# Seven visits one product later in their group, and the last head group's first output piece one period later

## The chip, the cores and the metric

The kernel runs on one core of a Trainium2 chip. The metric is the device time of one execution in microseconds (us); smaller is better. Before the change it was 687.55 us, the median of three runs.

## The reference

The program is one transformer block in bf16: sliding-window attention on a normalised input, a residual, and a dense layer with silu on the normalised result, again with a residual.

```python
qkv = x_ln @ wqkv                       # x_ln = layernorm(A_x), (2048, 1024)
q, k, v = 32 heads of 32 columns each
scores = (q @ k.T) * 32 ** -0.5
mask = (idx[:, None] - idx[None, :] >= 0) & (idx[:, None] - idx[None, :] < 256)
o = softmax(where(mask, scores, -1e9)) @ v
h = x + o @ wo
out = h + silu(layernorm(h) @ w1) @ w2  # w1 (1024, 3584), w2 (3584, 1024)
```

## The kernel before

The 2048 rows are four blocks of 512. The 32 heads are eight head groups of four heads; one unit of attention work is a head group `i = 8 * block + group` of one block. TensorE (PE in the profile) is kept busy with the dense products: first q, k and v of the four blocks (`qk_group`, L275, and `v_group`, L265), then the product with `wo` (`wo_group`, L296), then the dense layer (L801 and L829). Each such **group** is eight products of 128x512 into one PSUM bank, which VectorE (DVE) then copies out with a CAST (L277, L267) or an addition (L299).

The attention is threaded through the dense products by hand. The class `Attention` holds two tables, and `between` is called ahead of every dense product with a running count, `seen`: what a table holds for that count is issued first, in PE's own order. A PE instruction that has to wait therefore holds every product behind it.

- A **visit** (`visit`, L404 for its matmuls) computes scores with small matmuls of 32 rows by 64 columns, eight of them side by side, and then has ScalarE (ACT) take the exponential of each bank (L333 `exp_c`, L339 and L340 `exp_xy`, L442 `exp_0`) and GpSimd (POOL) apply the mask (L475). Blocks 1 to 3 are done in pairs of head groups, numbered `p` from 0 to 11. A **period** of 48 products belongs to each pair, from `t = 256 + 48 * p`, and holds three visits, `n` = 0, 1, 2, ahead of products `t+4`, `t+20` and `t+36`.
- A **piece** (`attn_piece`, L485) multiplies the exponentials of half a head group by v. VectorE follows with a reciprocal and a multiplication (L496, L497) that write the normalised output, and after the second half of a head group a transposing DMA is queued for the start of the next dense group (`late`).

Four PSUM banks serve all of that beside the four of `sc`. Three rotate among the dense groups; seen from a visit, `now` holds the group that is half done, `idle` is the bank that the next group will take, `behind` is the bank of the group just finished. The fourth, `out`, takes the results of the pieces and, at a visit, one unit of scores. A visit fills `sc`, `idle` and `out`, and where there is work for it `behind`:

```python
now = acc_n[0] % 3
idle, behind, out = (now + 1) % 3, (now + 2) % 3, 3
```

A first visit (`n` = 0) has a unit for `behind` only while `p < 8`: one head of the last two units of block 0 (`rest`, numbers 14 and 15), which belong to head group `G - 1` = 7. These are the visits with a **seventh bank** (four of `sc`, three more). Within the list of a visit with a seventh bank, the part for `behind` comes in the second half. Each of `rest`'s four heads is ready after two periods, so the two pieces of head group 7 of block 0 stand late: one in period 3 and one in period 7, ahead of product 32 of the period. Where they do, the piece that otherwise stands ahead of product 28 of the period (`t + 76` of the pair before) stands ahead of 27 (`t + 75`).

VectorE also does the layer norms of the next block between the groups: `ln1_steps` gives statistics, a reciprocal root by Newton steps, and four normalisations (`ln_norm`, L234), and the loop over `dense` appends one or two steps after every second group. For block 2 the four normalisations fall after groups 13 and 15, which end at `seen` = 432 and 448; period 3 begins at 400, period 4 at 448. An engine works its instructions in the order in which they were issued.

Of the kernel before, what the change touches and what calls it, by code (L numbers as in the profile page):

```python
# [54 lines left out]
def kernel(  # L55
# [22 lines left out]
    G = H // 4  # L78
# [56 lines left out]
    def xbuf(i):  # L135
        return r_e[:, 3072 + 5120 * (i % 2):5632 + 5120 * (i % 2)]

    def ybuf(i):
        return r_e[:, 5632 + 5120 * (i % 2):8192 + 5120 * (i % 2)]
# [165 lines left out]
    def mid_at(i, bank, h):  # L305
        return (h + 2) % 4 if bank == "X" and i % 2 else h
# [11 lines left out]
    def unit_xy(i, odd):  # L318
        q0 = odd * P
        mid, first, last = odd, odd - 2, odd + 2  # L320
        return [
            [(i, mid, q0, q0 + 320, 64), (i, last, q0 + 256, q0 + 384, 384), (i, first, q0, q0 + 64, 0)],
            [(i, mid, q0 + 64, q0 + 384, 128), (i, first, q0, q0 + 128, 0), (i, last, q0 + 320, q0 + 384, 448)],
        ]

    def unit_c(i):
        pair = (i, i + 1) if (i + 1) % 3 < (i + 2) % 3 else (i + 1, i)
        return [[(ii, kt, q * P, q * P + P, (n * 2 + m) * P)
                 for n, ii in enumerate(pair) for m, (kt, q) in enumerate(((-1, 0), (2, 3)))]] * 2

    def exp_c(i, h, bank):
        lo, hi = sorted(((i + 1) % 3, (i + 2) % 3))
        nc.scalar.activation(out=c_ring[:, lo:hi + 1:hi - lo, h, :], in_=four[bank].rearrange("p (n q) -> p n q", q=256),  # L333
                             func=ACT.Exp, scale=scale)

    def exp_xy(e, banks, h0, h1, m0=0):
        tri, mid = banks[:, :, 0:192], banks[:, :, 192:320]
        tri = bass.AP(tensor=tri.tensor, offset=tri.offset, ap=[*tri.ap[:2], [320, 2], tri.ap[2]])
        nc.scalar.activation(out=tri_of(e)[:, h0:h1, :, 64:256], in_=tri, func=ACT.Exp, scale=scale)  # L339
        nc.scalar.activation(out=full_of(e)[:, m0:m0 + h1 - h0, :], in_=mid, func=ACT.Exp, scale=scale)  # L340

    def select_xy(e, pair):
        four_q = e[:, 1024 * pair:1024 * (pair + 1)].rearrange("p (c q) -> p c q", q=256)
        select(four_q[:, :, 0:P], four_q[:, :, 64:64 + P], False)
        select(four_q[:, :, P:2 * P], four_q[:, :, P:2 * P], True)

    def visit(i, n):


        now = acc_n[0] % 3  # L350
        idle, behind, out = (now + 1) % 3, (now + 2) % 3, 3
        p = (i - G) // 2
        rest = (14 + p % 2, p // 2) if n == 0 and p < 8 else None
        c0, c1 = {1: (0, 2), 2: (1, 3)}.get(p // 2, (1, 2))
        if n == 0:
            own, e_own = unit_xy(i, 0), xbuf(i)
            more = [(c0, idle, unit_c(i)), (c1, out, unit_c(i))]
            if rest:
                more.append((rest[1], behind, unit_0(rest[0])))
        elif n == 1:  # L360
            own, e_own = unit_xy(i, 1), ybuf(i)
            more = [(5 - c1, idle, unit_c(i)), (0, out, unit_xy(i + 1, 0)), (1, behind, unit_xy(i + 1, 0))]
        else:
            own, e_own = unit_xy(i + 1, 1), ybuf(i + 1)
            more = [(1 - c0, idle, unit_c(i)), (2, out, unit_xy(i + 1, 0)), (3, behind, unit_xy(i + 1, 0))]
        scores(own, more, (idle, out)[:2 if n == 0 else 1], bool(rest))
        side = [h for h, _, unit in more if n and len(unit[0]) == 3]
        for h, bank, unit in more:
            if h in side:
                exp_xy(xbuf(i + 1), four[bank].rearrange("p (h q) -> p h q", h=1), h, h + 1, mid_at(i + 1, "X", h))  # L370
            elif len(unit[0]) == 4:
                exp_c(i, h, bank)
            else:
                exp_0(rest[0], h, bank)
        if side:
            select_xy(xbuf(i + 1), side[0] // 2)
        exp_xy(e_own, sc[:], 0, 4)
        for pair in range(2):
            select_xy(e_own, pair)
        if rest:  # L380
            m, h = rest
            select_0(m, h, h + 1)
            if m % 2:
                join_0(m, h, h + 1)

    def scores(own, more, ahead, longest=False):
        todo = []
        for h in range(4):
            for half in range(2):
                runs = [(sc[:, h, :], own[half])]  # L390
                for hh, bank, unit in more:
                    if hh == h:
                        runs.insert(0 if bank in ahead else 1, (four[bank], unit[half]))
                at = -sum(p[3] - p[2] for _, parts in runs for p in parts) if longest else 0
                for bank, parts in runs:
                    for p in parts:
                        todo.append((at, h, half, bank, p))
                        at += p[3] - p[2]
        todo.sort(key=lambda m: (m[0], m[4][2] - m[4][3] if longest else 0))
        for _, h, half, bank, (ii, kt, qa, qb, col) in todo:  # L400
            b, g = divmod(ii, G)
            t = b * 4 + kt
            r0, k0 = h * DH, (t % 4) * P + half * 64
            nc.tensor.matmul(  # L404
                bank[half * 64:half * 64 + 64, col:col + qb - qa],
                lhsT=kT[t // 4][r0:r0 + DH, g, k0:k0 + 64], rhs=qT[b][r0:r0 + DH, g, qa:qb],
                start=True, stop=True, tile_position=(r0, half * 64),
            )

    def unit_0(m):  # L410
        i, odd = divmod(m, 2)
        if odd:
            return [
                [(i, 1, 128, 448, 0), (i, 3, 384, 512, 320), (i, 2, 448, 512, 448)],
                [(i, 1, 128, 512, 0), (i, 3, 448, 512, 384), (i, 2, 448, 512, 448)],
            ]
        return [[(i, 0, 0, 320, 0), (i, 2, 256, 448, 320)], [(i, 0, 0, 384, 0), (i, 2, 320, 448, 384)]]
# [8 lines left out]
    def select_0(m, h0, h1):  # L426
        e = heads_0(m, h0, h1)

        if m % 2:
            select(e[:, :, 0:P], e[:, :, 0:P], True)  # L430
            select(e[:, :, 512:640], e[:, :, 320:448], True)
            select(e[:, :, 256:384], e[:, :, 256:384], False)
        else:
            select(e[:, :, 512:640], e[:, :, 256:384], False)
            select(e[:, :, 0:P], e[:, :, 0:P], True)
            select(e[:, :, 320:448], e[:, :, 320:448], True)

    def join_0(m, h0, h1):
        nc.gpsimd.tensor_copy(out=heads_0(m, h0, h1)[:, :, 384:448], in_=heads_0(m - 1, h0, h1)[:, :, 448:512])

    def exp_0(m, h, bank):
        nc.scalar.activation(out=heads_0(m, h, h + 1)[:, 0, 0:512], in_=four[bank], func=ACT.Exp, scale=scale)  # L442
# [71 lines left out]
    class Attention:  # L514


        def __init__(self):
            self.seen = 0
            self.visits, self.pieces = {}, {}
            at = [108, *range(132, 260, 16)]  # L520
            for k in range(8):
                self.visits[at[k]] = lambda k=k: visit_0(k)
            gaps = (1, 4), (1, 10), (2, 4), (3, 4), (4, 4), (4, 10), (5, 4), (5, 10), (6, 4), (6, 10), (7, 4), (7, 10), (8, 4), (8, 10)
            for d, (k, late) in enumerate(gaps):
                self.pieces[at[k] + late] = (d // 2, d % 2)
            for p in range((NB - 1) * G // 2):
                i, t = G + 2 * p, 256 + 48 * p
                for n in range(3):
                    self.visits[t + 4 + 16 * n] = lambda i=i, n=n: visit(i, n)
                for n in range(4):  # L530
                    self.pieces[t + (42, 47, 59, 75 if p in (2, 6) else 76)[n]] = (i + n // 2, n % 2)
            for k in range(2):
                self.pieces[256 + 48 * (4 * k + 3) + 32] = (G - 1, k)

        def between(self, kt):
            if self.seen in self.pieces:
# [169 lines left out]
    for g0 in range(0, G, 4):  # L706
        for w in range(2):
            for g in range(g0, g0 + 4):
                run_late()
                n = g0 * 2 + w * 4 + g % 4  # L710
# [171 lines left out]
```

## Time and profile before

| | before |
|---|---|
| median of 3 runs | 687.55 us (687.27 to 687.96) |
| the profiled execution's own time | 687.86 us |
| its span, first to last instruction | 686.1 us |
| PE busy | 672.4 us, 98% of the span |
| DVE, ACT, POOL busy | 291.7, 237.2, 163.0 us |
| granted TensorE clock | 1.000 |

A row of the timeline gives the start and the length in us, then engine, line, operation, what is written from what, and how many instructions are merged into the row; in brackets stands idle time of the engine ahead of the row and what ended it. Starts of matmuls are recorded; ends are modelled, and since matmuls are pipelined a row's end can lie after the start of the next. Some matmul records are missing from a trace. In this one a product of 128x512 starts 0.216 us after the one before it wherever nothing intervenes, and a gap of about 0.16 us called "issue" stands where such a record is missing.

### The profile page before, as it was taken

The page shows a single profiled execution, that of the slowest core. Times are in us where ns is not written, and L with a number is a line of the kernel's source. Part 1 is how long each engine was busy: PE and PEld are TensorE (multiplying, and loading weights), DVE is VectorE, ACT ScalarE, POOL GpSimd, SP SyncE. Part 2 cuts the span into 40 slices and gives each one's busy share as a digit, 9 for nine tenths or more (in the row PEclk, how much of TensorE's full clock was granted, in tenths as well). Part 3 has the DMA queues.
Part 4 walks back from the last instruction along what each step waited for, and adds up shares of the span by engine and source line. Part 5 has one row for each costly group of instructions (what it writes and reads, how often), then busy time and mean ns, then how long its engine had stood idle before and what let it go on. Part 6 is the DMA issues. An engine that isn't in the chain of part 4 may idle for free.

```text
span 686.1 us, 14503 instructions
## 1 busy us (share of the span) xinstructions
PE 672.4 (98%) x6097; PEld 338.1 (49%) x6200; DVE 291.7 (43%) x615; ACT 237.2 (35%) x405; POOL 163.0 (24%) x304
## 2 busy tenths in 40 slices
PE   9999999999999999999999999999999999999998
PEld 4445555555555555444444444444444444444445
DVE  5277745764444446634416133342244251344111
ACT  7337567667667674023300033200133100233000
POOL 1027966767776665000000000000000000000000
PEclk9999999999999999999999999999999999999999
DMA  8823124025633589865033310033200123100010
GB/s 275 261 53 89 33 55 102 19 41 90 190 88 70 166 250 266 194 237 189 1 104 113 67 39 1 0 93 78 76 1 0 40 83 86 39 1 0 32 38 24
DMA packets 77617, 61.50 MB, mean 90 GB/s; under 512 B 52464, under 2 KB 60656, under 8 KB 77552
## 3 DMA queue, kind: packets, MB, share of 16 engines
q1 hardware_dynamic: 77408, 60.31, 31.9%
q8 instruction: 48, 0.79, 0.5%
q10 hardware_dynamic: 144, 0.26, 0.1%
q14 instruction: 17, 0.14, 0.1%
HBM read 39.85 MB, written 8.39 MB: 70 GB/s over the span
## 4 chain that ended last, share of the span: by engine, by line
PE 97%; issue 1%; DMA 1%; DVE 0%; SPq 0%
PE hacc L801 16%; PE bank L275 16%; PE hacc L829 15%; PE bank L829 13%; PE bank L801 12%; PE bank L296 8%; PE bank L265 6%; PE bank L485 5%; PE sc L404 2%; PE bank L404 2%; PE bank L618 1%; DMA r_w<-in_A_wqkv_dram 1%; PE tp L265 1%; DVE r_o L234 0%; DVE r_a L277 0%
## 5 line engine op out<-in xcount | busy, mean ns | idle before, releaser
L475 POOL TENSOR_SCALAR_AFFINE_SELECT r_e<-r_e 128x512 bf16<-128x512 bf16 (+3 forms) x255 | 150.5, 604 | 105.6 <-ACT r_e L339 48.6
L829 PEld LDWEIGHTS <-r_a 128*128 128x128 bf16 x952 | 90.9, 98 | 103.0
L801 PEld LDWEIGHTS <-r_w 128*128 128x128 bf16 x896 | 87.7, 98 | 105.7
L829 PE MATMUL hacc<-r_a 128*128 128x512 bf16 (+2 forms) x523 | 103.2, 356 | 0.5
L829 PE MATMUL bank<-r_a 128*128 128x512 bf16 x411 | 91.3, 379 | 0.5
L801 PE MATMUL hacc<-r_e,r_w 128*128 128x512 bf16 x374 | 84.3, 379 | 0.5
L275 PEld LDWEIGHTS <-r_w 128*128 128x128 bf16 x512 | 45.4, 97 | 47.8
L801 PE MATMUL bank<-r_e,r_w 128*128 128x512 bf16 x286 | 64.3, 379 | 0.1
L277 DVE CAST r_a<-bank 128x512 bf16<-128x512 f32 x57 | 39.2, 688 | 50.7 <-PE bank L275 38.9
L275 PE MATMUL bank<-r_t,r_w 128*128 128x512 bf16 x233 | 58.1, 379 | 2.3 <-issue 1.6
L275 PE MATMUL bank<-r_w 128*128 128x512 bf16 x240 | 56.7, 379 | 1.5 <-issue 1.0
L296 PE MATMUL bank<-r_o,r_a 128*128 128x512 bf16 x242 | 56.8, 379 | 1.3 <-issue 0.8
L339 ACT ACTIVATE r_e<-sc 128x1536 bf16<-128x1536 f32 x36 | 53.4, 1484 | 0.0
L485 PEld LDWEIGHTS <-r_e 128*128 128x128 bf16 x1404 | 44.4, 96 | 14.6
L810 ACT ACTIVATE r_n<-bank 128x512 f32<-128x512 f32 x18 | 10.7, 597 | 117.0 <-PE bank L801 117.0
L333 ACT ACTIVATE r_e<-bank 128x512 bf16<-128x512 f32 x48 | 27.4, 596 | 59.5 <-PE bank L404 37.0
L485 PE MATMUL bank<-r_a,r_e 128*128 128x33 bf16 x1404 | 45.0, 178 | 0.1
L810 ACT ACTIVATE r_n<-hacc 128x512 f32<-128x512 f32 x24 | 14.3, 597 | 75.5 <-PE hacc L801 75.5
L844 DVE SCALAR_TENSOR_TENSOR r_t<-bank,r_t 128x512 bf16<-128x512 f32 x15 | 10.3, 684 | 66.6 <-PE bank L829 66.6
L296 PEld LDWEIGHTS <-r_a 128*128 128x128 bf16 x256 | 23.4, 97 | 25.7
L844 DVE SCALAR_TENSOR_TENSOR r_t<-hacc,r_t 128x512 bf16<-128x512 f32 (+2 forms) x19 | 12.0, 633 | 53.6 <-PE hacc L829 48.3
L404 PEld LDWEIGHTS <-r_a 32*64 32x64 bf16 x1856 | 23.9, 103 | 20.1 <-issue 19.8
(106 smaller groups left out, 610.1 us busy)
## 6 DMA issues: line engine op xcount, KB each, us to landing
r_w<-in_B_w_dram SPq DMA_DIRECT2D x8, 896.0 KB, 6.2
r_a<-in_B_w_dram SPq DMA_DIRECT2D x7, 1024.0 KB, 9.2
r_w<-in_A_wqkv_dram SPq DMA_DIRECT2D x4, 1024.0 KB, 8.3
r_t<-h_dram SPq DMA_DIRECT2D x16, 256.0 KB, 3.0
out_dram<-r_t SPq DMA_DIRECT2D x31, 128.0 KB, 1.7
r_e<-h_dram SPq DMA_DIRECT2D x3, 1024.0 KB, 5.7
r_o<-in_A_x_dram SPq DMA_DIRECT2D x11, 256.0 KB, 5.5
r_a<-in_A_x_dram SPq DMA_DIRECT2D x10, 256.0 KB, 4.2
```

The costliest lines, as they stand in the source:

```text
L265: nc.tensor.matmul(acc, lhsT=lnT_b[b % 2][:, kt, j * P:(j + 1) * P], rhs=wv[:, kt, c * 512:(c + 1) * 512], start=(kt == 0), stop=(kt == KT ...
L275: nc.tensor.matmul(acc, lhsT=wqk[:, kt, col0:col0 + P], rhs=lnT_b[b % 2][:, kt, :], start=(kt == 0), stop=(kt == KT - 1))
L277: copy(out=(qT, kT)[which][b][:, g, :], in_=acc)
L296: nc.tensor.matmul(acc, lhsT=qT[b][:, g, j * P:(j + 1) * P], rhs=wo[:, g, c * 512:(c + 1) * 512], start=(g == 0), stop=(g == G - 1))
L333: nc.scalar.activation(out=c_ring[:, lo:hi + 1:hi - lo, h, :], in_=four[bank].rearrange("p (n q) -> p n q", q=256), func=ACT.Exp, scale=scale)
L339: nc.scalar.activation(out=tri_of(e)[:, h0:h1, :, 64:256], in_=tri, func=ACT.Exp, scale=scale)
L404: nc.tensor.matmul(bank[half * 64:half * 64 + 64, col:col + qb - qa], lhsT=kT[t // 4][r0:r0 + DH, g, k0:k0 + 64], rhs=qT[b][r0:r0 + DH, g, ...
L475: nc.gpsimd.affine_select(out=dst, in_=src, pattern=[[0, n] for n in dst.shape[1:-1]] + [[sgn, P]], compare_op=ALU.is_ge if upper else ALU ...
L485: nc.tensor.matmul(o_ps[:, qt * 2 + hh, 0:VW], lhsT=chunk_of(i, bank, piece, pair * 2 + hh), rhs=v[:, b * 4 + kt, g * 4 + pair * 2 + hh, : ...
L801: nc.tensor.matmul(acc, lhsT=w1[:, kt, ft * P:(ft + 1) * P], rhs=ln2T[b][:, kt, :], start=(kt == 0), stop=(kt == KT - 1))
L810: nc.scalar.activation(out=th, in_=acc, func=ACT.Tanh, scale=0.5)
L829: nc.tensor.matmul(acc[:, 0:c1 - c0], lhsT=gT[:, ft, j * P:(j + 1) * P], rhs=w2[ft // 4][:, ft % 4, c0:c1], start=(ft == 0), stop=(ft == F ...
```

## The change

First visits of the pairs 1 to 7 are issued ahead of product 5 of their group instead of product 4. The first visit of pair 0, which also has a seventh bank, stays. The first piece of head group 7 of block 0 moves from period 3 to period 4, at the same place in the period; the second stays in period 7. Its neighbour ahead of product 27 moves along: the last piece of pair 2 goes to 28 of period 3, and that of pair 3 to 27 of period 4.

```diff
@@ -526,11 +526,11 @@
             for p in range((NB - 1) * G // 2):
                 i, t = G + 2 * p, 256 + 48 * p
                 for n in range(3):
-                    self.visits[t + 4 + 16 * n] = lambda i=i, n=n: visit(i, n)
+                    self.visits[t + (5 if n == 0 and 0 < p < 8 else 4) + 16 * n] = lambda i=i, n=n: visit(i, n)
                 for n in range(4):
-                    self.pieces[t + (42, 47, 59, 75 if p in (2, 6) else 76)[n]] = (i + n // 2, n % 2)
+                    self.pieces[t + (42, 47, 59, 75 if p in (3, 6) else 76)[n]] = (i + n // 2, n % 2)
             for k in range(2):
-                self.pieces[256 + 48 * (4 * k + 3) + 32] = (G - 1, k)
+                self.pieces[256 + 48 * (4, 7)[k] + 32] = (G - 1, k)
```

## The prediction

> **What bounds the kernel now.** I read the page first, for the engine that sets the end.
>
> ```profile
> span 686.1 us, 14503 instructions
> PE 672.4 (98%) x6097; PEld 338.1 (49%) x6200; DVE 291.7 (43%) x615; ACT 237.2 (35%) x405; POOL 163.0 (24%) x304
> PEclk9999999999999999999999999999999999999999
> PE 97%; issue 1%; DMA 1%; DVE 0%; SPq 0%
> ```
>
> PE is busy all through, at full clock, and 97% of the chain that ended last is PE. Whatever delays a PE start delays the end by as much, and only that counts. Next I asked what PE waited for.
>
> ```profile
> PE bank L275 <- issue: 2.5, 16, 0.2
> PE bank L404 <- DVE r_a L497: 0.9, 1, 0.9
> ```
>
> The "issue" gaps are missing records. One real wait is left: 0.9 us, once, ahead of a visit's matmul. This list counts from a modelled end, so I went on to starts. The chain around that wait, then PE and DVE at the visit (period 3, `n` = 2):
>
> ```profile
> 141.80 1.33 DVE r_o L234 x2
> 143.28 0.43 DVE r_a L497
> 143.75 0.25 PE bank L404
> ```
>
> ```profile
> 140.91 0.61 PE L485 MATMUL bank<-r_a 128*128 128x33 bf16 x18
> 142.31 0.32 PE L404 MATMUL sc<-r_a 32*64 32x320 bf16 x2
> 143.75 0.33 PE L404 MATMUL bank<-r_a 32*64 32x320 bf16 x4 [0.89 <-DVE r_a L497]
> 144.10 1.47 PE L275 MATMUL bank<-r_w 128*128 128x512 bf16 x5
> ```
>
> The piece of head group 7 fills `out` at 140.91. Its reciprocal and multiplication stand on DVE behind a CAST and two normalisations of 1.33 us together, so `out` is free at 143.28 + 0.42 = 143.70. The visit four products later needs `out` for scores; PE starts them at 143.75, a hand-over of 0.05 us, and everything behind on PE stood still.
>
> **The piece, one period later.** What does such a visit cost without the norms? The same arrangement stands in period 7, which isn't changed:
>
> ```profile
> 203.82 0.24 PE L404 MATMUL bank<-r_a 32*64 32x128 bf16 x2
> 204.41 1.47 PE L275 MATMUL bank<-r_t,r_w 128*128 128x512 bf16 x5
> 202.61 0.69 DVE L277 CAST r_a<-bank 128x512 bf16<-128x512 f32 x1 [0.35 <-PE bank L275]
> 203.45 0.42 DVE L497 TENSOR_TENSOR r_a<-bank,recip 128x256 bf16<-128x256 f32 x1
> ```
>
> There DVE goes from the CAST straight to the reciprocal, `out` is free at 203.87, and the visit takes 204.41 - 203.82 = 0.59 us to the next product. In period 3 it takes 144.10 - 142.31 = 1.79. The difference, **1.20 us**, is the whole price of the stall; 0.89 is only what shows beyond modelled ends. Which arrangement awaits the piece in period 4? DVE at that place now:
>
> ```profile
> 156.91 0.21 DVE L496 RECIPROCAL recip<-bank 128x8 f32<-128x8 f32 x1 [0.85 <-PE bank L485]
> 157.15 0.42 DVE L497 TENSOR_TENSOR r_n<-bank,recip 128x256 bf16<-128x256 f32 x1
> 157.71 0.69 DVE L277 CAST r_a<-bank 128x512 bf16<-128x512 f32 x1
> ```
>
> These are the answer to the piece ahead of product 28 and the CAST at the group's end, 480; in this loop the norms went after groups 13 and 15 (432 and 448), so none is queued at 480. The moved piece is 18 matmuls on PE and two instructions on DVE (0.62 us) wherever it stands; as a first half it issues no DMA, and it passes only casts, norms and other pieces' pairs on DVE. DVE then runs as in period 7, so I take that row: gain 1.20 us. Bounds: nothing, if a delay as long as the norms' met it there (the 1.33 us row); at most 1.20, since a visit can't be shorter than the undisturbed one. In period 3 the piece ahead of 27 falls back to 28; its pair stands on DVE ahead of the CAST and the norms, as in the rows of period 4 above, so it takes no stall over. The two neighbours that trade 27 and 28 stay inside their dense groups, so their transposing DMAs stay where they are among SP's; built, SP's, ACT's and POOL's orders are unchanged.
>
> **The seven visits.** No wait is listed for them, so I compared a visit with a seventh bank that waits (pair 3) with one that doesn't (pair 0), PE and DVE of each:
>
> ```profile
> 132.26 0.32 PE L404 MATMUL sc<-r_a 32*64 32x320 bf16 x2
> 132.59 0.32 PE L404 MATMUL bank<-r_a 32*64 32x384 bf16 x1
> 133.18 1.46 PE L275 MATMUL bank<-r_w 128*128 128x512 bf16 x6 [0.16 <-issue]
> 131.52 0.42 DVE L497 TENSOR_TENSOR r_n<-bank,recip 128x256 bf16<-128x256 f32 x1
> 131.86 0.68 DVE L277 CAST r_a<-bank 128x512 bf16<-128x512 f32 x1
> ```
>
> ```profile
> 88.68 0.32 PE L404 MATMUL sc<-r_a 32*64 32x320 bf16 x2
> 88.93 0.33 PE L404 MATMUL bank<-r_a 32*64 32x320 bf16 x2
> 89.49 1.89 PE L275 MATMUL bank<-r_t,r_w 128*128 128x512 bf16 x8 [0.16 <-issue]
> 88.07 0.68 DVE L277 CAST r_a<-bank 128x512 bf16<-128x512 f32 x1
> ```
>
> At pair 3 the piece ahead of product 47 of the period before puts its multiplication on DVE ahead of the CAST that empties `behind`, which ends at 132.54, 0.28 us into the visit; the scores for `behind` start at 132.59, 0.33 in. At pair 0 the CAST ends 0.07 in and they start 0.25 in. To the next recorded product (both lack one record, so like stands with like) it is 0.92 us against 0.81: **0.11 us** of waiting. The other changed visits, first and last of the seven:
>
> ```profile
> 102.32 0.32 PE L404 MATMUL sc<-r_a 32*64 32x320 bf16 x2
> 103.24 0.59 PE L275 MATMUL bank<-r_t,r_w 128*128 128x512 bf16 x2 [0.16 <-issue]
> 193.75 0.32 PE L404 MATMUL sc<-r_a 32*64 32x320 bf16 x2
> 194.68 0.59 PE L275 MATMUL bank<-r_t,r_w 128*128 128x512 bf16 x2 [0.16 <-issue]
> ```
>
> 0.92 and 0.93. One product later is 0.216 us (six products, 1.46 us with the last one's 0.38): the CAST would end 0.07 in, as at pair 0. Seven times 0.11 to 0.12 gives **0.8 us**, if all of the wait goes; at most that, and not less than nothing unless something else becomes late.
>
> What becomes late is the group after the visit. It takes `idle`, which ACT must first empty, and it now begins three products after the visit instead of four:
>
> ```profile
> 132.75 1.08 ACT L333 ACTIVATE r_e<-bank 128x512 bf16<-128x512 f32 x2 [1.79 <-PE bank L404]
> 117.82 1.08 ACT L333 ACTIVATE r_e<-bank 128x512 bf16<-128x512 f32 x2 [1.80 <-issue]
> 117.27 0.32 PE L404 MATMUL sc<-r_a 32*64 32x320 bf16 x2
> 120.60 0.63 ACT L340 ACTIVATE r_e<-sc 128x512 bf16<-128x512 f32 x1
> 122.13 0.34 PE L404 MATMUL sc<-r_a 32*64 32x320 bf16 x6
> L333 ACT ACTIVATE r_e<-bank 128x512 bf16<-128x512 f32 x48 | 27.4, 596 | 59.5 <-PE bank L404 37.0
> ```
>
> Its first product now starts at 133.18 + 3 x 0.216 = 133.83, which is 1.57 after the visit's start; later visit and vanished wait make it 1.57 - 0.22 - 0.11 = 1.24. The exponential of `idle` is the first of the two, 0.60 long, over 1.09 into the visit at pair 3, which starts at 132.26, and 1.15 into it at pair 2, which starts at 117.27. With a hand-over of 0.05, as DVE's above, that is 1.14 to 1.20: a margin of 0.10 to 0.04. I take nothing for it, since both rows clear it; if the hand-over from ACT is 0.1 longer it costs up to 0.06 each, 0.4 in all. Further on the cover is wide. The next piece, now six products behind the visit instead of seven, starts at 133.18 + 6 x 0.216 = 134.48 in the trace, 0.65 after the end of the exponential that frees `out` (132.75 + 1.08); it loses the same 0.33 of that and keeps 0.3. The following visit, 15 products on instead of 16, needs `sc`, free at 121.23; it starts at 122.13 and keeps 0.57 of its 0.90.
>
> The sum: 1.20 + 0.8 = **2.0 us** less of the profiled execution's 687.86 (the span of 686.1 and 1.8 around it, which the change leaves alone), hence 685.86. That execution is 0.31 above the median, and from the median 687.55 it is 685.5. A change of 0.2%, 1.4 us, is about what a measurement can tell from none.
>
> **The rivals.**
> 1. The seven visits give nothing: either their 0.11 us isn't the CAST (pair 0 works on other operands), or the group behind waits for `idle` by as much. For it: a margin of only 0.04 to 0.10 us. Against: the CAST's end and the start that it releases are 0.05 apart at pair 3, the same hand-over as at 143.75. Time: 687.55 - 1.20 = 686.35.
> 2. The stall goes along with the piece: some DVE work that the rows don't show meets it in period 4. Against: DVE's rows there. Time: 687.55 - 0.8 = 686.75.
> 3. Slower: the group behind isn't let go by the first exponential but by the last of the visit's three from bank to SBUF. The three stand 0.48 apart (1.08 - 0.60), so the last ends at 132.75 + 2 x 0.48 + 0.60 = 134.31, 2.05 into the visit; with 0.05 the group starts at 2.10 rather than 1.24: 0.86 x 7 = 6.0 lost, 2.0 won, 691.6. It turns the change into a loss once the group starts 0.29 us (2.0 / 7) past 1.24. Against it: at the visit at 132.26 that group starts at 133.83, just when the second exponential ends (132.75 + 1.08) and without the hand-over of 0.05, so it can have waited for the first at most.
> 4. Only time in which PE had no matmul under way can be won: the listed 0.89, so 687.55 - 0.89 = 686.66. Against: the next product's start is what the end hangs on, and it comes 1.79 after the visit's start instead of 0.59. The Trainium skill's page Perfetto Trace Analysis, section Optimization Strategy, has one find the gaps between slices of the bounding engine and what blocks there; the sum by that rule is this rival's. Its Tensor Engine timeline, though, calls a matmul's reported end an estimate, and the trace agrees: rows overlap the next start.
> 5. Nothing moves, 687.55. The built order shows the visits and the piece moved, so this is nearly out.
>
> **How the numbers follow.** My forecast, 685.5, has 0.80, with its own range of 685.0 to 686.1: the terms together between 1.7 and 2.05 us, and the three runs' spread of 0.3 to 0.4 each side. Rival 1 has 0.08, rival 2 0.06, rival 3 0.03, rival 4 0.02, rival 5 0.01. To 686.5 the range takes in rival 1 and leaves out 0.12 at the upper end. Faster by over 0.2% means below 686.17: the forecast's 0.80. Within 0.2%: rivals 1, 2, 4 and 5, 0.17. Slower: 0.03.
>
> **What would show it.** Right: PE's wait for L497 is gone; the visit `n` = 2 in period 3 takes about 0.59 to the next product, or 0.81 where a record is missing, and so does the one in period 4, where the multiplication follows the CAST with no L234 between; the seven visits take 0.81 instead of 0.92, the CAST ending some 0.07 into them, and the next group's first product follows the one before it by 0.216. Wrong: a start of that first product later than 0.216 after its predecessor, with an L333 ending just before (rival 1 or 3); L404 waiting for L497 at another place (rival 2); visits still at 0.92 with the CAST long over.

## The result and the profile after

| | before | after |
|---|---|---|
| median (9 runs each) | 687.55 us | 685.57 us |
| range | 687.27 to 688.12 | 685.36 to 686.77 |
| profiled execution, its span | 687.86, 686.1 us | 685.67, 684.0 us |

The ratio after to before is 0.9971, with a 95% interval of 0.9961 to 0.9981: 1.98 us less, where 2.0 was forecast. First PE's list of waits, after the change (waited for, then us in total, times, longest):

```profile
PE bank L275 <- issue: 2.7, 17, 0.2
PE bank L265 <- issue: 1.7, 11, 0.2
PE bank L199 <- DVE eps L179: 1.1, 1, 1.1
PE bank L296 <- issue: 0.8, 5, 0.2
```

The wait of L404 for L497 is gone and none has come. (The 1.1 us of L199 stands at the very start, at 1.13 us, before the change as after it.) The next fence is the visit `n` = 2 of period 3 on PE and on DVE.

```profile
141.31 0.32 PE L404 MATMUL sc<-r_a 32*64 32x320 bf16 x2
142.14 1.03 PE L275 MATMUL bank<-r_w 128*128 128x512 bf16 x4 [0.16 <-issue]
139.99 0.42 DVE L497 TENSOR_TENSOR r_n<-bank,recip 128x256 bf16<-128x256 f32 x1
140.55 0.69 DVE L277 CAST r_a<-bank 128x512 bf16<-128x512 f32 x1
141.16 1.64 DVE L234 TENSOR_SCALAR r_o<-r_o,st_a,rs_a 128x1024 bf16<-128x1024 bf16 x2
```

It took 1.79 us to the next product before; now it is 0.83 to the next recorded one, with one record missing (0.216). The norms are still there, but the multiplication that frees `out` ended at 140.41, ahead of them. The piece now stands in period 4:

```profile
155.21 0.61 PE L485 MATMUL bank<-r_a 128*128 128x33 bf16 x18
156.61 0.24 PE L404 MATMUL bank<-r_a 32*64 32x128 bf16 x2
157.20 0.82 PE L275 MATMUL bank<-r_w 128*128 128x512 bf16 x3
155.41 0.69 DVE L277 CAST r_a<-bank 128x512 bf16<-128x512 f32 x1 [0.35 <-PE bank L275]
156.01 0.20 DVE L496 RECIPROCAL recip<-bank 128x8 f32<-128x8 f32 x1
156.25 0.42 DVE L497 TENSOR_TENSOR r_a<-bank,recip 128x256 bf16<-128x256 f32 x1
```

CAST, reciprocal, multiplication, no L234 between: 0.59 us to the next product, as in period 7. Of the seven visits here is pair 3's, on PE, DVE and ACT:

```profile
132.01 0.32 PE L404 MATMUL sc<-r_a 32*64 32x320 bf16 x2
132.26 0.33 PE L404 MATMUL bank<-r_a 32*64 32x320 bf16 x2
132.84 1.24 PE L275 MATMUL bank<-r_w 128*128 128x512 bf16 x5 [0.16 <-issue]
131.40 0.68 DVE L277 CAST r_a<-bank 128x512 bf16<-128x512 f32 x1
132.51 1.08 ACT L333 ACTIVATE r_e<-bank 128x512 bf16<-128x512 f32 x2 [2.00 <-PE bank L404]
```

The CAST ends 0.07 us into the visit, the scores for `behind` start 0.25 in, and the next recorded product comes at 0.83 instead of 0.92. The five products are 0.216 apart (1.24 = 4 x 0.216 + 0.38), and the next group's first is the third of them, at 133.27: the first exponential, over at 133.11, holds nothing up.

Where the whole difference lies can be read from two rows of each run, the first visit of pair 0 and the last visit of all, since everything that the change touches stands between. First before, then after:

```profile
88.68 0.32 PE L404 MATMUL sc<-r_a 32*64 32x320 bf16 x2
263.18 0.24 PE L404 MATMUL bank<-r_a 32*64 32x128 bf16 x2
```

```profile
88.44 0.32 PE L404 MATMUL sc<-r_a 32*64 32x320 bf16 x2
261.00 0.24 PE L404 MATMUL bank<-r_a 32*64 32x128 bf16 x2
```

174.50 us became 172.56: **1.94 us less in this stretch**. The other 0.24 of the profiled pair's 2.19 arose ahead of the first visit, which the change doesn't touch; over all the profiles here that visit begins between 88.28 and 89.29. From the start of the last visit to the end of the time it is 424.67 to 424.71 in all nine profiled executions, so they differ by the stretch and by what lies ahead of it, and by nothing else. This start-up spread is probably also why the medians below wander by some tenths; each run's stretch stands beside its ratio for that reason. In the table, "less" is against the 174.50 of before.

| run | ratio to before (95%) | stretch, us | less, us |
|---|---|---|---|
| changed kernel | 0.9971 (0.9961 to 0.9981) | 172.56 | 1.94 |
| e1, visits only | 0.9994 (0.9985 to 1.0003) | 173.95 | 0.55 |
| e2, piece only | 0.9987 (0.9978 to 0.9996) | 173.31 | 1.19 |
| e3, norms later | 0.9973 (0.9962 to 0.9985) | 172.54 | 1.96 |
| e4, pieces ahead of 46 | 0.9984 (0.9975 to 0.9993) | 173.34 | 1.16 |
| e5, visits ahead of 6 | 0.9986 (0.9977 to 0.9994) | 173.46 | 1.04 |
| e6, visits ahead of 7 | 1.0009 (1.0000 to 1.0018) | 174.93 | -0.43 |
| e7, piece in period 5 | 0.9969 (0.9957 to 0.9980) | 172.54 | 1.96 |

### The profile page after: what moved, and what is told of

Same layout as the page of the kernel before. It is cut to its first block, busy times and chain, and to the rows that moved or that the text cites. A ratio compares the mean times of both kernels' runs of the same rounds, so it can differ in the third digit from the quotient of the medians.

```text
span 684.0 us, 14503 instructions
## 1 busy us (share of the span) xinstructions
PE 671.1 (98%) x6097; PEld 337.8 (49%) x6200; DVE 292.2 (43%) x615; ACT 237.0 (35%) x405; POOL 162.2 (24%) x304
## 4 chain that ended last, share of the span: by engine, by line
PE 98%; issue 1%; DVE 0%
PE hacc L801 16%; PE bank L275 16%; PE hacc L829 15%; PE bank L829 13%; PE bank L801 12%; PE bank L296 8%; PE bank L265 6%; PE bank L485 5%; PE sc L404 2%; PE bank L404 2%; PE bank L618 1%; PE tp L265 1%; PE bank L199 0%; PE tp L570 0%; PE tp L578 0%
## 5 line engine op out<-in xcount | busy, mean ns | idle before, releaser
L333 ACT ACTIVATE r_e<-bank 128x512 bf16<-128x512 f32 x48 | 27.4, 596 | 58.5 <-PE bank L404 36.3
L404 PEld LDWEIGHTS <-r_a 32*64 32x64 bf16 x1856 | 23.4, 103 | 18.8 <-issue 18.6
```

The source lines that it names most:

```text
L404: nc.tensor.matmul(bank[half * 64:half * 64 + 64, col:col + qb - qa], lhsT=kT[t // 4][r0:r0 + DH, g, k0:k0 + 64], rhs=qT[b][r0:r0 + DH, g, ...
```

## The experiments

The first two split the change. **e1, the visits alone:**

```diff
-                    self.visits[t + 4 + 16 * n] = ...
+                    self.visits[t + (5 if n == 0 and 0 < p < 8 else 4) + 16 * n] = ...
```

> The seven visits one product later, the first piece of head group 7 left in period 3. My theory: the visits stop waiting for the CAST that empties the bank `behind`, 7 times about 0.11 us, and the stall of the visit in period 3 stays at about 1.2 us: 687.55 - 0.77 = 686.8, and in the trace PE waits once for L497. Rival (the seven visits give nothing, the whole gain is the piece): 687.55. Rival (the whole gain is the visits): 685.6.

687.50 us against 687.83 for before on that chip: 0.4 less by the ratio, with an interval from 1.0 less to 0.2 more, which can't tell 0.77 from nothing. The stretch gave 0.55. The seven visits' wait was gone (first two rows: pair 3's visit takes 0.59 us, no record missing), but the stall in period 3 had grown. That visit on PE and DVE follows, and as the last row the norms before the change:

```profile
132.85 0.32 PE L404 MATMUL sc<-r_a 32*64 32x320 bf16 x2
133.44 1.25 PE L275 MATMUL bank<-r_w 128*128 128x512 bf16 x5
...
142.59 0.32 PE L404 MATMUL sc<-r_a 32*64 32x320 bf16 x2
144.26 0.33 PE L404 MATMUL bank<-r_a 32*64 32x320 bf16 x4 [1.12 <-DVE r_a L497]
144.60 0.61 PE L275 MATMUL bank<-r_w 128*128 128x512 bf16 x2
141.99 1.64 DVE L234 TENSOR_SCALAR r_o<-r_o,st_a,rs_a 128x1024 bf16<-128x1024 bf16 x2
...
141.72 1.41 DVE L234 TENSOR_SCALAR r_o<-r_o,st_a,rs_a 128x1024 bf16<-128x1024 bf16 x2
```

The stalled visit takes 2.01 us instead of 1.79, because the two norms run for 1.64 us instead of 1.41. So 0.77 was won and 0.22 given back, which leaves the 0.55. The changed kernel has the same long norms (141.16 above) and nobody waits for them there.

**e2, the piece alone** (the tables of the changed kernel, with all visits at `t + 4 + 16 * n`):

> The piece in period 4, the seven visits ahead of product 4 as before. My theory: the stall of 1.18 to 1.20 us behind the two norms goes and nothing else: 686.35; the seven visits still show 0.92 us to the next recorded product, 0.70 where no record is missing. Rival (the whole gain is the visits): 687.55. Rival (the two parts only work together): 687.55 here and in the run with the visits alone.

The stretch is 1.19 us shorter, the ratio 0.9987. The visit of pair 3 in e2, no record missing:

```profile
132.32 0.32 PE L404 MATMUL sc<-r_a 32*64 32x320 bf16 x2
133.02 1.47 PE L275 MATMUL bank<-r_w 128*128 128x512 bf16 x6
```

0.70 us, the wait for the CAST still in it. Both parts give something on their own, so neither "all is the piece" nor "all is the visits" holds.

**e3, the norms moved instead of the piece.** The piece stays in period 3, the visits are one later, and in the loop over blocks 2 and 3:

```diff
-                for _ in range(1 if len(steps) > 8 else 2):
+                for _ in range(1 if len(steps) > 8 else {13: 0, 15: 4}.get(n, 2)):
```

> The seven visits one product later; the piece of head group 7 stays in period 3, but VectorE's two normalisations after group 13 of block 2 go after group 15, where four then stand together. On every other engine the order is that of the run with the visits alone. My theory: the stall was VectorE's queue and nothing about period 3, so the wait for L497 goes and the time is that of the changed kernel, 685.6 (up to 0.3 more if four norms in a row, some 2.5 us, hold up a CAST that PE then waits for). Rival (period 3 itself is a bad place, for the exponentials or the masks of its pieces): 686.8, with the wait still there.

1.96 us less in the stretch, as much as the change itself. The visit of period 3 on PE, and DVE's order in e3:

```profile
142.24 0.32 PE L404 MATMUL sc<-r_a 32*64 32x320 bf16 x2
142.84 0.60 PE L275 MATMUL bank<-r_w 128*128 128x512 bf16 x2
141.03 0.69 DVE L277 CAST r_a<-bank 128x512 bf16<-128x512 f32 x1 [0.35 <-PE bank L275]
141.64 0.20 DVE L496 RECIPROCAL recip<-bank 128x8 f32<-128x8 f32 x1
141.87 0.43 DVE L497 TENSOR_TENSOR r_a<-bank,recip 128x256 bf16<-128x256 f32 x1
147.81 2.22 DVE L234 TENSOR_SCALAR r_o<-r_o,st_a,rs_a 128x1024 bf16<-128x1024 bf16 x4
```

PE's order is that of e1, the piece is in period 3, and the visit takes 0.60. The stall was the place of two norms in VectorE's queue; nothing about the period did it. Four norms in a row held up no one here.

**e4, the CAST freed from the other side.** The visits stay ahead of product 4; the pieces in front of them go one product earlier (the piece of head group 7 in period 4):

```diff
-                    self.pieces[t + (42, 47, 59, 75 if p in (3, 6) else 76)[n]] = ...
+                    self.pieces[t + (42, 46 if p < 7 else 47, 59, 75 if p in (3, 6) else 76)[n]] = ...
```

> The piece in period 4, the seven visits ahead of product 4 as before, but the pieces ahead of product 47 in the seven periods before those visits go ahead of 46. That gives VectorE the reciprocal and the multiplication 0.216 us earlier and leaves the visit where it was. My theory: the visit waited for the CAST only because that pair stood ahead of it on VectorE, so the scores for `behind` start about 0.25 us into the visit instead of 0.33 and the seven visits win their 0.77 us; but the piece now follows its neighbour ahead of 42 after four products, and may wait about 0.05 us for the multiplication that empties `out`, 7 times: 685.6 to 686.0. Rival (it is the visit's place in the group that matters, or work of the seventh bank itself): no gain over the run with the piece alone, 686.35.

By time it looks like the rival: 1.16 us less, against e2's 1.19. PE and DVE ahead of pair 3's visit tell why:

```profile
129.01 1.02 PE L275 MATMUL bank<-r_w 128*128 128x512 bf16 x4
129.99 0.75 PE L485 MATMUL bank<-r_a,r_e 128*128 128x33 bf16 x24
131.97 0.32 PE L404 MATMUL sc<-r_a 32*64 32x320 bf16 x2
132.22 0.33 PE L404 MATMUL bank<-r_a 32*64 32x320 bf16 x2
132.57 0.60 PE L275 MATMUL bank<-r_w 128*128 128x512 bf16 x2
129.51 0.42 DVE L497 TENSOR_TENSOR r_n<-bank,recip 128x256 bf16<-128x256 f32 x1
```

The scores for `behind` do start 0.25 us into the visit, which takes 0.60 instead of e2's 0.70, with the visit where it was: the wait was for the CAST. But the piece could have started at 129.01 + 4 x 0.216 = 129.87 and starts at 129.99, 0.06 after the multiplication at 129.93 that frees `out` for it. Those 0.12 us, seven times, are what was won. I had put that wait at 0.05, from the rows of the other piece; it was more than twice that.

**e5 and e6, the visits later still,** ahead of 6 and of 7 (the 5 in the table replaced), find the point at which the group behind becomes late.

> As the changed kernel, but the seven visits two products later than before (ahead of product 6). My theory: the CAST is long over, so nothing is won by it; the group after the visit now begins two products behind it, nominally 1.02 to 1.04 us after the visit's start, and its bank `idle` is free only when the first exponential ends, at 1.09 to 1.14, plus a hand-over of 0.05: a wait of 0.11 to 0.17 us seven times, about 0.9 us, 686.5. Rival (that group waits for the second exponential, over at 1.58 to 1.63): 0.6 us seven times, about 690. Rival (no ScalarE wait at all): 685.6.

> As the changed kernel, but the seven visits three products later than before (ahead of product 7). My theory: one product less of cover than with 6, so each wait grows by a whole product, 0.216 us, to 0.33 to 0.39: about 2.4 us in all, 688.0, slower than before. That slope (1.5 us more than with 6) is what a release at a fixed time after the visit's start gives. Rival (second exponential): 691.5. Rival (no ScalarE wait): 685.6.

PE and ACT at pair 3's visit in e6, ahead of 7:

```profile
133.43 0.32 PE L404 MATMUL sc<-r_a 32*64 32x320 bf16 x2
134.58 0.81 PE L275 MATMUL bank<-r_w 128*128 128x512 bf16 x3 [0.48 <-ACT r_e L333]
133.93 1.09 ACT L333 ACTIVATE r_e<-bank 128x512 bf16<-128x512 f32 x2 [2.43 <-PE bank L404]
```

The first exponential ends at 133.93 + 0.60 = 134.53, the group starts at 134.58, and PE's list names ACT's L333 as what was waited for. In e5, ahead of 6, the wait is there but below what the list counts; it shows as a row that is too long (pair 3, then pair 2):

```profile
134.16 1.13 PE L275 MATMUL bank<-r_w 128*128 128x512 bf16 x4 [0.16 <-issue]
119.11 1.20 PE L265 MATMUL bank<-r_w 128*128 128x512 bf16 x4 [0.16 <-issue]
```

Four products take 3 x 0.216 + 0.38 = 1.03; these rows are 0.10 and 0.17 longer, the 0.11 and 0.17 expected. Against the changed kernel's stretch e5 lost 0.90 us (0.9 expected) and e6 2.37 (2.4 expected). The release is fixed by the first exponential, and ahead of 5 is the last place that clears it.

**e7, the piece in period 5:**

```diff
-                    ... 75 if p in (3, 6) else 76 ...
-                self.pieces[256 + 48 * (4, 7)[k] + 32] = (G - 1, k)
+                    ... 75 if p in (4, 6) else 76 ...
+                self.pieces[256 + 48 * (5, 7)[k] + 32] = (G - 1, k)
```

> As the changed kernel, but the piece two periods later than before (period 5, and the neighbour ahead of product 27 along with it), where VectorE has no norms either. My theory: the same as the changed kernel, 685.6. Rival (period 4 is special, or later is better still): off by more than 0.3.

685.71 us, and a stretch of 172.54 beside 172.56: no difference. Periods 4 and 5, both without norms at that place, do equally well.

None of the runs points to a faster version: neither the list nor the starts show a visit of the changed kernel that still waits, and e3 and e7 only reach the same time in other ways.

## Why the prediction was right, step by step

- **The stall in period 3, 1.20 us.** e2 gave 1.19 for it alone. That the price is the difference of starts and not the listed 0.89 is shown by the same number, so rival 4 falls. Undisturbed, this visit takes 0.60 (e3) and not the 0.59 of its twin in period 7, which makes the stall 1.19 rather than 1.20. The mechanism, two norms ahead of the reciprocal on DVE, is shown by e3.
- **That it wouldn't follow the piece** (rival 2): the rows of period 4 above, and e7.
- **The seven visits, 0.8 us.** Measured 0.75 (1.94 - 1.19) or 0.77 (e1's 0.55 and the 0.22 that it gave back). The waits of 0.11 to 0.12 went whole in the visits of even pairs; odd pairs' went to 0.82 or 0.83 instead of pair 0's 0.81. Their unit 15 has more small matmuls (46 in the visit's records instead of 44), a difference that the wait had covered. That the CAST was the cause is shown by e4, from the other side.
- **What becomes late next.** The margin, 0.04 to 0.10 us with a hand-over of 0.05, was taken from DVE's hand-over since no row had ACT's. e6 measured ACT's: 0.05. It was enough by the 0.04 that the nearest pair had. Rival 1 and rival 3 had their place here; e5 and e6 show that the first exponential is what counts, and that one product more would have cost 0.9 us.
- **What the prediction didn't see:** moving the visits lengthens the first of the two norms by 0.23 us (the last section shows how). It cost nothing only because the piece was moved as well, which was luck; e1 shows the cost without that. Its "one real wait is left" also passed over the 1.1 us of L199 in the same list, which ends ahead of all that was changed.

## What to carry to other kernels

On an engine that sets the end, compare start to start with a twin of the same work that doesn't wait: a list of idle gaps missed seven waits of 0.11 us wholly and a quarter of a stall of 1.20. Before moving a step to free a wait, work out which release the next step down the line has, and how much margin it keeps: here a room of 0.37 to 0.43 us held the 0.33 that the change took of it, and one product more would have given back almost half of the gain. A short step that others wait for should not be queued behind long ones that nobody waits for; either may be moved.

## What the runs showed of the hardware

VectorE's norm of 128x1024 bf16 takes very different times. In e3, where four stand in a row, here are the durations of the 13 norms on this tile (ns, minimum, median and maximum), the first, the second and the fourth of the four, and the last of GpSimd's masks there:

```profile
L234 DVE TENSOR_SCALAR r_o<-r_o,st_a,rs_a x13: 533/547/857, 12.4 to 149.5; 128x1024 bf16<-128x1024 bf16 x13
147.81 0.54 DVE L234 TENSOR_SCALAR r_o<-r_o,st_a,rs_a 128x1024 bf16<-128x1024 bf16 x1
148.26 0.86 DVE L234 TENSOR_SCALAR r_o<-r_o,st_a,rs_a 128x1024 bf16<-128x1024 bf16 x1
149.49 0.53 DVE L234 TENSOR_SCALAR r_o<-r_o,st_a,rs_a 128x1024 bf16<-128x1024 bf16 x1
147.94 0.90 POOL L475 TENSOR_SCALAR_AFFINE_SELECT r_e<-r_e 128x512 bf16<-128x512 bf16 x1
```

A norm that meets no mask takes 0.53 to 0.55 us, and a 128x512 mask that meets no norm about 0.64. The mask above begins beside the first norm and takes 0.90: it ends at 148.84, 0.49 after that norm's end. The second norm begins beside the mask and takes 0.86: it ends at 149.12, 0.28 after the mask's end. In all nine profiles every norm that takes 0.61 us or more ends 0.28 us after an instruction of GpSimd, and every 128x512 mask that begins beside a norm and outlasts it ends 0.49 after that norm. The Trainium skill's page SBUF — State Buffer, section Who interferes with whom, has VectorE and GpSimd share one pair of ports under an exclusive lock. The trace agrees: an end at a fixed time after the other's end, wherever the two met, is what one would see if the later one waited within its own row. So the 0.58 us for which the second norm and the mask stand side by side need not be work on both.

This also tells why the norms of period 3 took 1.41 us before and 1.64 in e1. Here is the first of the two with the mask that it meets, before and then in e1; the second took 0.85 in both.

```profile
141.72 0.64 DVE L234 TENSOR_SCALAR r_o<-r_o,st_a,rs_a 128x1024 bf16<-128x1024 bf16 x1
141.44 0.64 POOL L475 TENSOR_SCALAR_AFFINE_SELECT r_e<-r_e 128x512 bf16<-128x512 bf16 x1
141.99 0.87 DVE L234 TENSOR_SCALAR r_o<-r_o,st_a,rs_a 128x1024 bf16<-128x1024 bf16 x1
141.95 0.63 POOL L475 TENSOR_SCALAR_AFFINE_SELECT r_e<-r_e 128x512 bf16<-128x512 bf16 x1
```

The norm ends 0.28 us after the mask in both (142.36 and 142.08, 142.86 and 142.58), but in e1 it began 0.04 into the mask instead of 0.28, and so ran longer. GpSimd begins its masks 3.48 us after the period's first visit in both runs and works on without a pause past the norms, while the norms come 9.46 us after that visit before and 9.14 in e1. The other runs fit: this norm took 0.64 to 0.66 with the visits ahead of 4 (before, e2, e4), 0.87 ahead of 5 (the changed kernel, e1, e7) and 0.98 ahead of 6 and 7. No run moved the masks alone.
